# mLSTM cell and mixture of depths on one core: another order of work within a chunk

## The chip, the core and the metric

The kernel runs on one core of a Trainium2 chip. A core has five engines that run their own instruction queues in order: TensorE (PE in the profile, its weight loads PEld), VectorE (DVE), ScalarE (ACT), GpSimd (POOL) and SyncE (SP), which here only starts DMA transfers. They meet through semaphores. The metric is the device time of one execution in microseconds.

## The reference

Two stages in a row. The first is an mLSTM cell over 4 batches, 8 heads, 768 tokens and a head size of 40; its output, heads side by side, is a row of 320 per token. The second picks in every batch the 128 tokens with the highest score, and adds to each of these rows a gated two-layer network.

```python
# mLSTM, for every token t (B, H in front)
m_new  = max(f[t] + m, i[t])
f_stab = exp(f[t] + m - m_new);  i_stab = exp(i[t] - m_new);  m = m_new
C = f_stab * C + i_stab * outer(v[t], k[t])
n = f_stab * n + i_stab * k[t]
y[t] = sigmoid(o_gate[t]) * (C @ q[t]) / max(abs(n . q[t]), 1)

# mixture of depths, for every batch b, on x = y with the heads side by side (768 x 320)
scores = x @ w_gate
top = indices of the 128 largest scores
out = x
out[top] = x[top] + sigmoid(scores[top]) * (relu(x[top] @ w1) @ w2)     # w1 320x1024, w2 1024x320
```

## The kernel before

The tokens are cut into 24 chunks of 128: n = 6 b + c, chunk c of batch b. Within a chunk the recurrence is a masked 128 x 128 product per head; from chunk to chunk goes the state C. All products are float32. The gates of three chunks of all batches lie in one tile of 96 rows (chunk, batch, head), so there are two groups of them.

```python
def load_gates(eng, dst, src, g):                      # f_sb, i_sb: [96, 128]
    eng.dma_start(out=dst[g], in_=src.rearrange("b h (c p) -> c (b h) p", p=L)[3 * g:3 * g + 3])

load_gates(nc.sync, f_sb, f_gate, 0);   load_gates(nc.scalar, i_sb, i_gate, 0)
load_gates(nc.scalar, f_sb, f_gate, 1); load_gates(nc.scalar, i_sb, i_gate, 1)
...
def warm(n):                    # n fillers on TensorE: a bf16 product that nobody reads (pw)
def scans(g):                   # VectorE: running sums and maxima of the gates of a group (FM, a)
def ends(g), carry(g), carried(g), level(g, pm)        # the stabilizer m carried from chunk to chunk
def operands(u, c):             # TensorE pO, ScalarE a_o, VectorE M_o: factors whose product is log W
def turned(n):                  # TensorE transposes k and q (pt), ScalarE copies them (T)
def gated(n):                   # ScalarE: so = tanh(o_gate / 2) + 1
def weights(b, c):              # TensorE pW, ScalarE W = exp(pW), [128, 8, 128]
def causal(W):                  # GpSimd: affine_select zeroes W above the diagonal, in two halves
def scaled_v(b, c, v1):         # GpSimd: wv = v * column
def products(T):                # TensorE: pS = k q^T for 8 heads
def weighted(pS, W):            # VectorE: P = pS * W, in two halves
def decay(b, c):                # GpSimd: C of the next chunk = C * column
def exchange(b, c, qk, T, wv):  # TensorE: pI = C q, pC = k wv; VectorE: num = pI * column, then C += pC (c = 0: copy)
def within(P, v1):              # TensorE: pH = P v
...
def norm(num, pH, so):
    nc.vector.tensor_tensor(out=num, in0=num, in1=pH[:, :, 0:D1], op=OP.add)          # not for c = 0
    # two small VectorE operations: den = 2 max(|n q|, 1)
    nc.vector.reciprocal(out=rec, in_=den)
    nc.gpsimd.tensor_tensor(out=sor, in0=so, in1=rec.unsqueeze(2).to_broadcast([128, H, D]), op=OP.mult)
    return num, sor

def result(b, c, num, sor, sc):
    nc.vector.tensor_tensor(out=x..., in0=num[:, :, 0:D], in1=sor, op=OP.mult)
    nc.sync.dma_start(out=out[b, c * L:(c + 1) * L, :], in_=x)
    nc.vector.tensor_tensor_reduce(out=scr, in0=x, in1=wg, ..., accum_out=sc[:, c:c + 1])   # the score

def spread(u, sc, sb):          # TensorE pb, ScalarE sb: the scores of chunk u along the free axis
def compare(u, sc, sb, ge, cnt):# VectorE ge: which scores are at least as high, and how many
def columns_of(ge):             # TensorE pcol: 21 one-column products, counts the other way round
def ranks(pcol, cnt):           # two small VectorE operations
def select(sel, rank, t0, t1):  # VectorE: sel = (rank == 0 .. 127), 128 x 768
def gather(b, sel, token):      # TensorE pidx, VectorE idx, then GpSimd's indirect DMA: xe <- out[idx]

class Layers:                   # the two layers of one batch on its 128 rows
    def enter(self):            # TensorE pX (transposes of xe), ScalarE xeT
    def gate(self):             # VectorE scre, ScalarE exp, VectorE +1 and reciprocal
    def first(self, f0, f1):    # TensorE ph, ScalarE relu hT after every fourth f; 8 f in all
    def second(self, f0, f1):   # TensorE py
    def leave(self):            # VectorE ye, GpSimd's indirect DMA: out[idx] <- ye
```

The step of one chunk, in the order of each engine's queue:

```python
def ranking(b, c):
    if b > 0 and c == 1:
        rank = ranks(columns_of(state[b - 1][1][2]), state[b - 1][1][3])
        select(sel[b - 1], rank, 0, NT)
    elif b > 0 and c == 2:
        picked[b - 1] = gather(b - 1, sel[b - 1], token)

def layer(b, c):
    if c < 3:
        if b > 1:  layers[b - 2].second(3 * c, min(3 * c + 3, NFC))
        else:      warm(3)
    elif b == 0:   warm(3)
    elif b < B - 1:
        if c > 3:  layers[b - 1].first(3 * c - 10, 3 * c - 7)
    elif c == 4:   layers[b - 1].first(2, 6)
    elif c == 5:
        layers[b - 1].first(6, NFC);  layers[b - 1].second(0, 4)

def entered(b, c):
    if b > 0 and c == 3:
        layers[b - 1] = Layers(b - 1, *picked[b - 1]);  layers[b - 1].enter();  layers[b - 1].first(0, 2)

def step(n):
    load(n + AHEAD)                                    # k, q, v, o_gate of chunk n + 4: four DMAs
    P = weighted(pS[n], W[n])
    W[n + 2] = weights(*steps[n + 2])
    num = exchange(b, c, qk, T[n], wv[n])
    ranking(b, c);  layer(b, c)
    pH = within(P, v1)
    spread(pc, ...)                                    # of the chunk before
    turned(n + 2);  gated(n + 2)
    pS[n + 1] = products(T[n + 1])
    num, sor = norm(num, pH, so)
    decay(*steps[n + 1])
    causal(W[n + 2]);  stated(n + 2)                   # stated: scaled_v
    compare(pc, ...)                                   # of the chunk before
    result(b, c, num, sor, state[b][0])
    entered(b, c)
    if b > 0 and c == 3:  layers[b - 1].gate()
    if b > 1 and c == 2:  layers[b - 2].leave()
    if n + 3 < NT:        operands(0, n + 3)
    if 3 <= n < 3 + NT:   operands(1, n - 3)
```

Ahead of the steps stands a start with the work of chunk 0 and the gates; behind them a tail: the last spread and compare, `own.second(4, NFC)` of batch 2, ranks, select, products with sel, the gather and both layers of batch 3, and the last scatter.

Of the kernel before, what the change touches and what calls it, by code (L numbers as in the profile page):

```python
# [27 lines left out]
def kernel(  # L28
# [59 lines left out]
    i_sb = [gate.tile([NR, L], FP, name=f"i_sb{g}") for g in range(2)]  # L88

    def load_gates(eng, dst, src, g):  # L90
        eng.dma_start(out=dst[g], in_=src.rearrange("b h (c p) -> c (b h) p", p=L)[3 * g:3 * g + 3])

    load_gates(nc.sync, f_sb, f_gate, 0)
    load_gates(nc.scalar, i_sb, i_gate, 0)
    load_gates(nc.scalar, f_sb, f_gate, 1)
    load_gates(nc.scalar, i_sb, i_gate, 1)
    earlier = const.tile([128, NT * L], BF, name="earlier")
    nc.gpsimd.memset(earlier, 1.0)
    ident = const.tile([128, 128], FP, name="ident")
# [69 lines left out]
    def warm(n):  # L169

        pw = ps_h.tile([128, 4 * L], FP, name="pw", tag="h")
        for _ in range(n):
            nc.tensor.matmul(pw, earlier[:, 0:128], earlier[:, 0:4 * L], start=True, stop=True)  # L173
# [233 lines left out]
    def columns_of(ge):  # L407

        pcol = ps_m.tile([128, NT], FP, name="pcol", tag="m")
        for t in reversed(range(NT)):  # L410
            for u in reversed(range(t, NT)):
                nc.tensor.matmul(pcol[:, t:t + 1], ge[:, GE[u] + t * L:GE[u] + (t + 1) * L], ones_b, start=(u == NT - 1),
                                 stop=(u == t))
        return pcol

    def ranks(pcol, cnt):


        rank = mod.tile([128, NT], FP, name="rank")
        nc.vector.tensor_tensor(out=rank, in0=cnt, in1=later, op=OP.add)  # L420
        nc.vector.tensor_tensor(out=rank, in0=rank, in1=pcol, op=OP.subtract)
        return rank

    def select(sel, rank, t0, t1):
        nc.vector.tensor_tensor(out=sel[:, t0:t1], in0=iota_f.unsqueeze(1).to_broadcast([128, t1 - t0, K_]),
                                in1=rank[:, t0:t1].unsqueeze(2).to_broadcast([128, t1 - t0, K_]), op=OP.is_equal)

    def gather(b, sel, token):
        pidx = ps_m.tile([K_, 1], FP, name="pidx", tag="m")
        for t in range(NT):  # L430
            nc.tensor.matmul(pidx, sel[:, t, :], token[:, t:t + 1], start=(t == 0), stop=(t == NT - 1))
        idx = mod.tile([K_, 1], U32, name="idx")
        nc.vector.tensor_scalar(out=idx, in0=pidx, scalar1=float(b * S), scalar2=None, op0=OP.add)
        xe = xe_t[b % 2]
        nc.gpsimd.indirect_dma_start(out=xe[0:K_, 0:DM], out_offset=None, in_=rows(b),
                                     in_offset=bass.IndirectOffsetOnAxis(ap=idx, axis=0),
                                     bounds_check=(b + 1) * S - 1, oob_is_err=False)
        return idx, xe

    class Layers:  # L440
# [14 lines left out]
        def gate(self):  # L455
            scr = mod.tile([K_, DM], FP, name="scre", bufs=1)
            self.g = g = mod.tile([K_, 1], FP, name="g")
            nc.vector.tensor_tensor_reduce(out=scr, in0=self.xe[0:K_, 0:DM], in1=wg[0:K_], scale=1.0, scalar=0.0,
                                           op0=OP.mult, op1=OP.add, accum_out=g)
            nc.scalar.activation(out=g, in_=g, func=AF.Exp, scale=-1.0)  # L460
            nc.vector.tensor_scalar(out=g, in0=g, scalar1=1.0, scalar2=None, op0=OP.add)
            nc.vector.reciprocal(out=g, in_=g)

        def first(self, f0, f1):
            for f in range(f0, f1):
# [41 lines left out]
    def stated(n):  # L507
        wv[n] = scaled_v(*steps[n], loaded[n][1])

    def ranking(b, c):  # L510

        if b > 0 and c == 1:
            rank = ranks(columns_of(state[b - 1][1][2]), state[b - 1][1][3])
            sel[b - 1] = mod.tile([128, NT, K_], HF, name="sel", bufs=1)
            select(sel[b - 1], rank, 0, NT)
        elif b > 0 and c == 2:
            picked[b - 1] = gather(b - 1, sel[b - 1], token)

    def layer(b, c):
# [17 lines left out]
    def entered(b, c):  # L537
        if b > 0 and c == 3:
            layers[b - 1] = Layers(b - 1, *picked[b - 1])
            layers[b - 1].enter()  # L540
            layers[b - 1].first(0, 2)

    def step(n):
        b, c = steps[n]
        qk, v1, so = loaded[n]
        load(n + AHEAD)
        P = weighted(pS[n], W[n])
        if n + 2 < N:
            W[n + 2] = weights(*steps[n + 2])
        num = exchange(b, c, qk, T[n], wv[n])  # L550
        ranking(b, c)
        layer(b, c)
        pH = within(P, v1)
# [8 lines left out]
        if n + 1 < N:  # L562
            decay(*steps[n + 1])
        if n + 2 < N:
# [7 lines left out]
        if b > 0 and c == 3:  # L572
# [12 lines left out]
    load(2)  # L585
    load(3)
    load(4)
    pS = {}
    warm(7)

    scans(0)
    ends(0)
    split(0, 1, 0, nc.vector.tensor_copy, nc.vector)
    carry(0)
    warm(2)
    pm = carried(0)
    split(0, 1, 1, nc.vector.tensor_copy, nc.vector)
# [4 lines left out]
    turn(loaded[0][0], 0, T[0])  # L602
    operands(0, 0)
    scales(0)
    turn(loaded[0][0], 1, T[0])
    warm(1)
    W[0] = weights(0, 0)
    pS[0] = products(T[0])
    operands(0, 1)
    columns(0)  # L610
    warm(2)
    causal(W[0])
    stated(0)

    gated(0)
    scans(1)
    W[1] = weights(0, 1)
    P = weighted(pS[0], W[0])
    split(1, 1, 0, nc.gpsimd.tensor_copy, nc.gpsimd)
    split(1, 1, 1, nc.gpsimd.tensor_copy, nc.gpsimd)  # L620
    ends(1)
    warm(2)
    exchange(0, 0, loaded[0][0], T[0], wv[0])
    carry(1)
    turned(1)
    operands(0, 2)
    causal(W[1])
    stated(1)
    pm = carried(1)
    pH = within(P, loaded[0][1])  # L630
    pS[1] = products(T[1])
    level(1, pm)
    W[2] = weights(0, 2)
    num, sor = norm(None, pH, loaded[0][2])
    split(1, 0, 0, nc.scalar.copy, nc.vector)
    decay(0, 1)
    causal(W[2])
    stated(2)
    split(1, 0, 1, nc.scalar.copy, nc.vector)
    result(0, 0, num, sor, state[0][0])  # L640
    scales(1)
    gated(1)
    turned(2)
# [89 lines left out]
```

## Time and profile before

| | |
|---|---|
| time, median of 3 runs | 234.72 us (232.8 to 236.89) |
| span of the profiled execution | 235.5 us |
| mean granted TensorE clock | 0.896 |
| first pH after the start (chunk 0) | 23.46 us |
| pH of chunk 6, 12, 18 | 77.22, 124.64, 166.89 us |
| last spread (pb) | 208.51 us |

Busy time is given by engine, and in windows by stage. A row of a group tells the line of the kernel, the engine, the operation, what it writes and reads (names of tiles), the shapes, how often, then busy microseconds and the mean in nanoseconds of one, then the time that the engine had stood idle ahead of it and what ended that. The chain of work goes back from the last instruction, at each step to what released it; a piece has its start, its length and what it was.

### The profile page before, as it was taken

The numbers are of one execution on the slowest core, as the hardware profiler recorded it, in microseconds if no ns is written. First come the engines' busy times: TensorE is split into PE (matmuls) and PEld (weight loads), VectorE is DVE, ScalarE is ACT, GpSimd is POOL, SyncE is SP. The second block draws the span as 40 slices with busy tenths as digits, with TensorE's granted clock in tenths as the row PEclk, the third lists the DMA queues.
The fourth block names the chain that finished last, engine by engine and source line by source line (L and its number), as shares of the span: only waits on it lengthen the run. The fifth ranks groups of instructions, "written<-read, shape, count | busy, mean of one in ns | idle before, by whom it ended". The sixth has DMA issues, their size and how long they took to land.

```text
span 235.5 us, 6469 instructions
## 1 busy us (share of the span) xinstructions
PE 201.2 (85%) x2611; PEld 159.6 (68%) x2611; DVE 156.0 (66%) x414; ACT 93.9 (40%) x212; POOL 104.6 (44%) x152
## 2 busy tenths in 40 slices
PE   5799889669778898589999997999999799858991
PEld 1356757457556886477887776788787679637980
DVE  3644273875888898886678789857888885642010
ACT  3643282343355353533565344465434541100020
POOL 6035320860556536731546477534647951021101
PEclk9755556997999799979999999999999999958998
DMA  4899964748599999999089987949992110000100
GB/s 72 144 159 148 98 101 42 112 76 97 154 132 200 157 212 190 152 125 140 25 120 140 144 125 135 168 53 141 131 134 49 58 57 3 28 31 29 30 0 28
DMA packets 105674, 24.37 MB, mean 103 GB/s; under 512 B 100460, under 2 KB 105068, under 8 KB 105644
## 3 DMA queue, kind: packets, MB, share of 16 engines
q1 hardware_dynamic: 104963, 22.50, 65.4%
q0 software_dynamic: 384, 1.31, 2.0%
q8 instruction: 20, 0.33, 0.7%
q10 hardware_dynamic: 297, 0.15, 0.2%
q14 instruction: 10, 0.08, 0.1%
HBM read 19.37 MB, written 4.59 MB: 102 GB/s over the span
## 4 chain that ended last, share of the span: by engine, by line
PE 58%; DVE 15%; issue 13%; POOL 5%; DMA 4%; ACT 2%; POOLq 1%
PE pH L367 12%; PE pS L313 9%; PE ph L469 8%; PE pt L271 7%; PE pIC L339 5%; PE py L478 4%; DVE x L387 4%; PE pIC L345 3%; PE pw L173 3%; POOL sor L382 2%; PE pW L291 2%; DVE scr L390 2%; DMA f_sb<-in_f_gate_dram 2%; PE pb L396 2%; DVE P L319 2%
## 5 line engine op out<-in xcount | busy, mean ns | idle before, releaser
L382 POOL TENSOR_TENSOR sor<-so,rec 128x320 f32<-128x320 f32 x24 | 23.3, 969 | 87.5 <-DVE rec L380 82.2
L367 PEld LDWEIGHTS pH<-v,P 128*64 128x64 f32 x768 | 28.4, 153 | 21.0 <-DVE P L319 8.3
L367 PE MATMUL pH<-v,P 128*64 128x64 f32 x768 | 32.0, 242 | 11.9 <-DVE P L319 6.0
L297 POOL TENSOR_SCALAR_AFFINE_SELECT W<-W 128x512 f32<-128x512 f32 x48 | 37.1, 794 | 9.1 <-ACT W L292 9.1
L397 ACT COPY sb<-pb 128x128 f32<-128x128 f32 x24 | 6.4, 266 | 71.4 <-PE pb L396 71.4
L292 ACT ACTIVATE W<-pW 128x512 f32<-128x512 f32 x48 | 26.0, 594 | 12.0 <-PE pW L291 7.6
L319 DVE TENSOR_TENSOR P<-pS,W 128x512 f32<-128x512 f32 x48 | 30.6, 677 | 0.0
L272 ACT COPY T<-pt 128x512 f32<-128x512 f32 x48 | 26.1, 588 | 9.9 <-PE pt L271 9.9
L313 PE MATMUL pS<-T 64*128 64x128 f32 x384 | 29.7, 297 | 0.0
L271 PE MATMUL pt<-ident,qk 128*128 128x128 f32 x192 | 29.0, 300 | 0.7 <-ACT W L292 0.7
L387 DVE TENSOR_TENSOR x<-num,sor 128x320 f32<-128x320 f32 x20 | 20.3, 1017 | 12.5 <-POOL sor L382 12.5
L313 PEld LDWEIGHTS pS<-T 64*128 64x128 f32 x384 | 24.9, 199 | 4.6 <-issue 4.4
L271 PEld LDWEIGHTS pt<-ident,qk 128*128 128x128 f32 x192 | 24.9, 156 | 1.7 <-ACT W L292 1.2
L469 PE MATMUL ph<-xeT,w 128*128 128x128 f32 x192 | 24.1, 280 | 2.0 <-ACT xeT L453 1.7
L469 PEld LDWEIGHTS ph<-xeT,w 128*128 128x128 f32 x192 | 22.2, 192 | 3.3 <-ACT xeT L453 2.4
L478 PE MATMUL py<-w,hT 128*128 128x320 f32 x64 | 21.4, 480 | 0.0
L374 DVE TENSOR_TENSOR num<-num,pH 128x328 f32<-128x328 f32 x20 | 9.9, 496 | 16.2 <-PE pH L367 16.0
L390 DVE CUSTOM_DVE_ANT_0 scr<-x,wg 128x320 f32<-128x320 f32 x24 | 17.1, 712 | 0.8
L304 POOL TENSOR_TENSOR wv<-v,cols 128x328 f32<-128x328 f32 x20 | 16.2, 811 | 2.6 <-DVE cols L245 2.6
L403 DVE SCALAR_TENSOR_TENSOR ge<-sb,sc,earlier 128x128 bf16<-128x128 f32 (+5 forms) x24 | 16.0, 667 | 1.0 <-ACT sb L397 0.9
L339 PE MATMUL pIC<-C,T 128*64 128x82 f32 x320 | 16.4, 246 | 0.0
L339 PEld LDWEIGHTS pIC<-C,T 128*64 128x64 f32 x320 | 13.0, 140 | 4.1 <-issue 2.5
(124 smaller groups left out, 269.5 us busy)
## 6 DMA issues: line engine op xcount, KB each, us to landing
qk<-in_k_dram SPq DMA_DIRECT2D x24, 160.0 KB, 3.8
qk<-in_q_dram SPq DMA_DIRECT2D x24, 160.0 KB, 5.0
v<-in_v_dram SPq DMA_DIRECT2D x24, 160.0 KB, 4.9
so<-in_o_gate_dram SPq DMA_DIRECT2D x24, 160.0 KB, 4.5
out_dram<-x SPq DMA_DIRECT2D x24, 160.0 KB, 1.9
w<-in_moe_w_dram SPq DMA_DIRECT2D x2, 640.0 KB, 4.5
w<-in_moe_w_dram SPq DMA_DIRECT2D x2, 512.0 KB, 4.0
w<-in_moe_w_dram SPq DMA_DIRECT2D x1, 256.0 KB, 3.9
```

The costliest lines, as they stand in the source:

```text
L271: nc.tensor.transpose(pt[:, p, :], qk[:, j, 2 * p:2 * p + 2, :].rearrange("s a d -> s (a d)"), ident)
L272: nc.scalar.copy(out=T[:, j], in_=pt)
L292: nc.scalar.activation(out=W[:, h0:h0 + 4, :], in_=pW, func=AF.Exp)
L297: nc.gpsimd.affine_select(out=W[:, h0:h0 + 4, :], in_=W[:, h0:h0 + 4, :], compare_op=OP.is_ge, fill=0.0, base=0, pattern=[[0, 4], [1, L]], ...
L313: nc.tensor.matmul(pS[j][:, p, :], T[e, 0, p, :], T[e, 1, p, :], start=True, stop=True)
L319: nc.vector.tensor_tensor(out=P[:, :, j, :], in0=pS[j], op=OP.mult, in1=W.rearrange("p (n a) t -> p n a t", a=2)[:, :, j, :])
L339: nc.tensor.matmul(pI[t, 2 * p * D1:2 * (p + 1) * D1], T[:, 1, p, t], C[:, p].rearrange("e a d -> e (a d)"), start=True, stop=True)
L367: nc.tensor.matmul(pH[t, 2 * p + j, :], P[:, p, j, t], v1[:, 2 * p + j, :], start=True, stop=True)
L382: nc.gpsimd.tensor_tensor(out=sor, in0=so, in1=rec.unsqueeze(2).to_broadcast([128, H, D]), op=OP.mult)
L387: nc.vector.tensor_tensor(out=x.rearrange("p (h d) -> p h d", d=D), in0=num[:, :, 0:D], in1=sor, op=OP.mult)
L469: nc.tensor.matmul(self.ph[:, f % 4, :], w1[:, j, f * 128:(f + 1) * 128], self.xeT[:, j, :], start=(j == 0), stop=(j == NDC - 1))
L478: nc.tensor.matmul(self.py, self.hT[:, f, :], w2[:, f, :], start=(f == 0), stop=(f == NFC - 1))
```

## The change

The order within a chunk changes, and with it the place of the second stage's work. GpSimd does the selects, wv and the decay of the state as soon as their inputs can be there, and the product with the output gate, sor, last. The ranking of a batch goes to the end of the next batch's chunk 0 (it was in chunk 1), the gather to chunk 1 (2), the entry of the layers and the gate to chunk 2 (3); the closing two operations of the gate become `gated()`, at chunk 3. The first layer then takes chunks 3 to 5. The last batch does five second products ahead of the tail instead of four. The gates are loaded in pieces of 32 rows, the second group by SyncE behind chunk 0. In the start VectorE's operations of chunk 0 take another order, and the fillers stand elsewhere.

```diff
     def load_gates(eng, dst, src, g):
-        eng.dma_start(out=dst[g], in_=src.rearrange("b h (c p) -> c (b h) p", p=L)[3 * g:3 * g + 3])
+        for c in range(3):
+            t = slice((3 * g + c) * L, (3 * g + c + 1) * L)
+            eng.dma_start(out=dst[g][c * BH:(c + 1) * BH], in_=src[:, :, t].rearrange("b h p -> (b h) p"))
 ...
-    load_gates(nc.scalar, f_sb, f_gate, 1)
-    load_gates(nc.scalar, i_sb, i_gate, 1)
 ...
-    def ranking(b, c):
+    def layer(b, c):
         if b > 0 and c == 1:
-            rank = ranks(columns_of(state[b - 1][1][2]), state[b - 1][1][3])
-            sel[b - 1] = mod.tile([128, NT, K_], HF, name="sel", bufs=1)
-            select(sel[b - 1], rank, 0, NT)
+            picked[b - 1] = gather(b - 1, sel[b - 1], token)
         elif b > 0 and c == 2:
-            picked[b - 1] = gather(b - 1, sel[b - 1], token)
+            layers[b - 1] = Layers(b - 1, *picked[b - 1])
+            layers[b - 1].enter()
         if c < 3: ...                                   # as before
         elif b == 0:
             warm(3)
+        elif c == 3:
+            layers[b - 1].gated()
+            layers[b - 1].first(0, 3)
         elif b < B - 1:
-            if c > 3:
-                layers[b - 1].first(3 * c - 10, 3 * c - 7)
+            layers[b - 1].first(3 * c - 9, min(3 * c - 6, NFC))
         elif c == 4:
-            layers[b - 1].first(2, 6)
-        elif c == 5:
-            layers[b - 1].first(6, NFC)
-            layers[b - 1].second(0, 4)
-    def entered(b, c): ...
+            layers[b - 1].first(3, 7)
+        else:
+            layers[b - 1].first(7, NFC)
+            layers[b - 1].second(0, 5)
 ...
     def step(n):
         P = weighted(pS[n], W[n])
             W[n + 2] = weights(*steps[n + 2])
+            causal(W[n + 2])
+            stated(n + 2)
         num = exchange(b, c, qk, T[n], wv[n])
-        ranking(b, c)
+            decay(*steps[n + 1])
         layer(b, c)
         ...
             pS[n + 1] = products(T[n + 1])
         num, sor = norm(num, pH, so)
-            decay(*steps[n + 1])
-            causal(W[n + 2])
-            stated(n + 2)
         compare(pc, *state[pb][1])
+        if b > 0 and c == 0:
+            pcol = columns_of(state[b - 1][1][2])
         result(b, c, num, sor, state[b][0])
-        entered(b, c)
-        if b > 0 and c == 3:
+        if b > 0 and c == 0:
+            rank = ranks(pcol, state[b - 1][1][3])
+            sel[b - 1] = mod.tile([128, NT, K_], HF, name="sel", bufs=1)
+            select(sel[b - 1], rank, 0, NT)
+        elif b > 0 and c == 2:
             layers[b - 1].gate()
-        if b > 1 and c == 2:
-            layers[b - 2].leave()
+            if b > 1:
+                layers[b - 2].leave()
 ...
     load(0)
+    load_gates(nc.sync, f_sb, f_gate, 1)
+    load_gates(nc.sync, i_sb, i_gate, 1)
     load(1)
 ...                                                     # the start: fillers warm(...) in order
-    warm(7); scans; ends; split; carry; warm(2); carried; ...; turn; operands; scales; turn; warm(1); weights; products; columns; warm(2)
+    warm(8); scans; ends; warm(2); split; carry; carried; warm(1); ...; turn; warm(1); operands; scales; turn; columns; weights; warm(1); products
 ...                                                     # chunk 0: P ahead of W[1], causal(W[1]) and turned(1) ahead of exchange,
-    scans(1); W[1] = weights(0, 1); P = weighted(...); split; ends(1); warm(2); exchange(0, 0, ...); carry(1); turned(1); ...
+    scans(1); P = weighted(...); W[1] = weights(0, 1); split; causal(W[1]); ends(1); turned(1); warm(1); exchange(0, 0, ...); carry(1); ...
 ...                                                     # the tail
-    own.second(4, NFC)
+    own.second(5, NFC)
     last.gate()
+    last.gated()
```

More of the change, by code (lines that the diff above doesn't have):

```diff
@@ L460, in gate, with gated @@
             nc.scalar.activation(out=g, in_=g, func=AF.Exp, scale=-1.0)
-            nc.vector.tensor_scalar(out=g, in0=g, scalar1=1.0, scalar2=None, op0=OP.add)
-            nc.vector.reciprocal(out=g, in_=g)
+        def gated(self):
+            nc.vector.tensor_scalar(out=self.g, in0=self.g, scalar1=1.0, scalar2=None, op0=OP.add)
+            nc.vector.reciprocal(out=self.g, in_=self.g)
         def first(self, f0, f1):
@@ L508, in stated @@
         wv[n] = scaled_v(*steps[n], loaded[n][1])
-    def ranking(b, c):
+    def layer(b, c):
         if b > 0 and c == 1:
-            rank = ranks(columns_of(state[b - 1][1][2]), state[b - 1][1][3])
-            sel[b - 1] = mod.tile([128, NT, K_], HF, name="sel", bufs=1)
-            select(sel[b - 1], rank, 0, NT)
+            picked[b - 1] = gather(b - 1, sel[b - 1], token)
         elif b > 0 and c == 2:
-            picked[b - 1] = gather(b - 1, sel[b - 1], token)
-    def layer(b, c):
+            layers[b - 1] = Layers(b - 1, *picked[b - 1])
+            layers[b - 1].enter()
         if c < 3:
@@ L527, in layer @@
             warm(3)
+        elif c == 3:
+            layers[b - 1].gated()
+            layers[b - 1].first(0, 3)
         elif b < B - 1:
-            if c > 3:
-                layers[b - 1].first(3 * c - 10, 3 * c - 7)
+            layers[b - 1].first(3 * c - 9, min(3 * c - 6, NFC))
         elif c == 4:
-            layers[b - 1].first(2, 6)
-        elif c == 5:
-            layers[b - 1].first(6, NFC)
-            layers[b - 1].second(0, 4)
-    def entered(b, c):
-        if b > 0 and c == 3:
-            layers[b - 1] = Layers(b - 1, *picked[b - 1])
-            layers[b - 1].enter()
-            layers[b - 1].first(0, 2)
+            layers[b - 1].first(3, 7)
+        else:
+            layers[b - 1].first(7, NFC)
+            layers[b - 1].second(0, 5)
     def step(n):
@@ L549, in step @@
             W[n + 2] = weights(*steps[n + 2])
+            causal(W[n + 2])
+            stated(n + 2)
         num = exchange(b, c, qk, T[n], wv[n])
-        ranking(b, c)
+        if n + 1 < N:
+            decay(*steps[n + 1])
         layer(b, c)
@@ L561, in step @@
         num, sor = norm(num, pH, so)
-        if n + 1 < N:
-            decay(*steps[n + 1])
-        if n + 2 < N:
-            causal(W[n + 2])
-            stated(n + 2)
         compare(pc, *state[pb][1])
+        if b > 0 and c == 0:
+            pcol = columns_of(state[b - 1][1][2])
         if c == 0:
@@ L570, in step @@
         result(b, c, num, sor, state[b][0])
-        entered(b, c)
-        if b > 0 and c == 3:
+        if b > 0 and c == 0:
[3 more added lines that the diff above has]
+        elif b > 0 and c == 2:
             layers[b - 1].gate()
-        if b > 1 and c == 2:
-            layers[b - 2].leave()
+            if b > 1:
+                layers[b - 2].leave()
         if n + 3 < NT:
@@ L588 @@
     pS = {}
-    warm(7)
+    warm(8)
     scans(0)
     ends(0)
+    warm(2)
     split(0, 1, 0, nc.vector.tensor_copy, nc.vector)
     carry(0)
-    warm(2)
     pm = carried(0)
+    warm(1)
     split(0, 1, 1, nc.vector.tensor_copy, nc.vector)
@@ L602 @@
     turn(loaded[0][0], 0, T[0])
+    warm(1)
     operands(0, 0)
@@ L605 @@
     turn(loaded[0][0], 1, T[0])
+    columns(0)
+    W[0] = weights(0, 0)
     warm(1)
-    W[0] = weights(0, 0)
     pS[0] = products(T[0])
     operands(0, 1)
-    columns(0)
-    warm(2)
     causal(W[0])
@@ L616 @@
     scans(1)
+    P = weighted(pS[0], W[0])
     W[1] = weights(0, 1)
-    P = weighted(pS[0], W[0])
     split(1, 1, 0, nc.gpsimd.tensor_copy, nc.gpsimd)
     split(1, 1, 1, nc.gpsimd.tensor_copy, nc.gpsimd)
+    causal(W[1])
     ends(1)
-    warm(2)
+    turned(1)
+    warm(1)
     exchange(0, 0, loaded[0][0], T[0], wv[0])
     carry(1)
-    turned(1)
+    pH = within(P, loaded[0][1])
     operands(0, 2)
-    causal(W[1])
+    pm = carried(1)
+    pS[1] = products(T[1])
+    num, sor = norm(None, pH, loaded[0][2])
     stated(1)
-    pm = carried(1)
-    pH = within(P, loaded[0][1])
-    pS[1] = products(T[1])
+    decay(0, 1)
     level(1, pm)
     W[2] = weights(0, 2)
-    num, sor = norm(None, pH, loaded[0][2])
     split(1, 0, 0, nc.scalar.copy, nc.vector)
-    decay(0, 1)
+    result(0, 0, num, sor, state[0][0])
+    split(1, 0, 1, nc.scalar.copy, nc.vector)
     causal(W[2])
     stated(2)
-    split(1, 0, 1, nc.scalar.copy, nc.vector)
-    result(0, 0, num, sor, state[0][0])
     scales(1)
```

## The prediction

> **What bounds the kernel now.** I read the page first, then the chain of work that ended last in order of time, the groups by line with shapes kept apart, and the windows by stage, and I followed a few steps of one 128-token chunk instruction by instruction. The page says which engine is fullest, and that the granted TensorE clock is half in the slices from about 12 to 35 us:
>
> ```profile
> PE 201.2 (85%) x2611; PEld 159.6 (68%) x2611; DVE 156.0 (66%) x414; ACT 93.9 (40%) x212; POOL 104.6 (44%) x152
> ...
> PEclk9755556997999799979999999999999999958998
> ```
>
> The stages follow (columns: length, busy time of each engine, granted clock, DMA). "Chunk n" is the n-th of 24; the boundaries are starts of pH.
>
> ```profile
> 0.00:37.40 37.40, 30.32 (x217) 18.76 (x217) 18.40 (x59) 16.97 (x39) 12.79 (x32) 0.62 0.96 120
> ...
> 55.60:92.10 36.50, 30.77 (x497) 24.96 (x498) 29.92 (x75) 17.25 (x40) 19.91 (x28) 0.94 0.98 155
> 92.10:124.60 32.50, 28.49 (x395) 24.20 (x395) 25.00 (x61) 15.20 (x33) 14.92 (x18) 0.95 0.80 127
> 124.60:166.90 42.30, 40.28 (x611) 33.39 (x610) 34.13 (x90) 21.10 (x46) 24.36 (x29) 1.00 0.86 126
> ```
>
> From 124.6 us on PE is 95% busy: little is left there. From 37 to 124 it is not, although it runs three filler matmuls (pw) per chunk that compute nothing. The chain shows why; this is chunk 4 to chunk 5:
>
> ```profile
> 67.98 0.77 PE pw L173 x3
> 68.75 1.58 issue
> 70.33 1.24 PE pH L367 x32
> ```
>
> PE stands 1.58 us in front of pH, which needs P = pS x W from VectorE. So this stage is **VectorE's loop**: P, num, C, then num+pH, den, rec, ge, a wait for GpSimd's sor, x, scr, and P again. Two members of it are stretched:
>
> ```profile
> L387 DVE TENSOR_TENSOR x<-num,sor 128x320 f32<-128x320 f32 x20 | 20.3, 1017 | 12.5 <-POOL sor L382 12.5
> L387 DVE TENSOR_TENSOR x<-pH,sor 128x320 f32<-128x320 f32 x4 | 1.9, 485 | 1.2 <-POOL sor L382 1.2
> L390 DVE CUSTOM_DVE_ANT_0 scr<-x,wg 128x320 f32<-128x320 f32 x24 | 17.1, 712 | 0.8
> ```
>
> The same x takes 1017 ns with both inputs in SBUF and 485 ns with one in PSUM; in chunk 22, where GpSimd has nothing left to do, the SBUF form takes 0.49 too. GpSimd works exactly there because its queue runs sor, decay (C), two affine selects (W), wv, and sor waits for rec: 82.2 us of waiting in all, after which everything behind it falls on x and scr. Worst is chunk 8, behind the gather:
>
> ```profile
> 96.03 2.89 DVE x L387
> 98.92 0.03 issue
> 98.95 0.49 DVE scr L390
> ```
>
> PE idles 3.44 us there, and the next matmuls come out at half clock (pt x8 takes 1.70 instead of 0.87).
>
> **What the Trainium skill says.** GPSIMD Engine Reference, Key points: GpSimd shares its SBUF interfaces with VectorE, and they contend when the VectorE instruction has two SBUF inputs. The trace agrees (1017 against 485 ns). DMA: Bandwidth & Descriptors, the section on why a DMA increments its semaphore by 16: a DMA is spread over the largest k up to 16 that divides the slowest dimensions of both sides. The old gate load has 3 on one side and 96 on the other, which would be 3 engines; its 48 KB take 4.65 us on the chain, 160 KB of x take 1.9 to land. The trace agrees without showing the engines. TensorE: Matmul & The Clock Gate, What's actually happening: half clock after an idle window of about 3.4 us, full after a busy one. The trace agrees loosely: half from 8.9 to 39.6 us although PE is about 90% busy by the page's modelled ends, so the threshold can't be read off it. The DMA page, Issuing engines are not separate DMA queues: moving the second gate loads from ScalarE to SyncE changes only who spends the issue time, seen here as 0.4 to 1.9 us an issue.
>
> **The change, part by part**, from 234.7 us.
>
> *GpSimd's order.* The selects, wv and decay come ahead of sor. They need W of chunk n+2 (ScalarE ends it about 1 us after the old sor ends) and C of this chunk, so they fall under P, num and C, which have one input in PSUM. Their sum is 1.5 + 0.74 + 0.73 = 3.0 us, begun some 3.2 us after one pH ends, done before the next rec. Then x falls from 1.01 to 0.49 and scr from 0.80 to 0.49: 0.83 us per chunk in VectorE's loop (0.7 where there is no decay). sor beside ge (0.72 alone, up to 1.39) stays. Chunks 1 to 8 run on that loop or on the similar one through M_o and pW (in chunks 1 and 2): seven intervals, 54.7 us, at 0.83 = 5.8; another 0.7 for half-clock pieces (75 to 80 us stands at 0.72) as PE idles less: **-6.5**.
>
> *Chunks 8 to 12 of batch 1.* x of 2.88 loses 2.4 (0.49 left), and the half-clock matmuls of 100.8 to 104.6 lose 1.5 (pH 0.6, pt 0.8, pb 0.1). The entry of the layers moves a chunk forward, so PE no longer waits 0.57 for xeT, which ScalarE copies while PE has its transposes. Two more exposed waits of about 0.3 are worth 0.5: **-5**. As a check, PE's need here is four times 4.7 plus 6.4 of first, 1.7 of second, under 27 against 32.6 used.
>
> *Batches 2 and 3.* Ranks and select (0.17 + 0.17 + 0.96 = 1.3 us of VectorE) move from chunk 1 to chunk 0, which has no num and so a light VectorE; the gather moves to chunk 1, the entry to chunk 2; the gate keeps its 0.9 scre but leaves chunk 3. Exposed now per batch: 1.28 in front of pH of chunk 3, 0.57 for xeT, 0.16 for idx, 2.0 together, twice 4.0. The gather is issued after C and lands 3.4 us later, about 4 us before pX wants it. After the change VectorE needs about 5.5 us from pH of chunk 2 to P, PE 6.1 (0.2 + 0.87 + 1.09 + 0.32 + 1.18 + 2.4 of first), so PE waits no more. Less half a microsecond for the fifth second matmul moved in, and half kept for leftovers: **-3**.
>
> *The tail.* One of four second matmuls leaves the stretch at half clock (208.5 to 212.5): two passes at 0.53, **-1**. The rest of the tail is as it was.
>
> *The start.* The gates load as 3 DMAs of 32 rows. Three issues of some 0.65 end at 2.8, landing some 1.9 later gives 4.6 against 5.46: **-1**. The fillers are moved (14 to 14) to where PE idled between the gate steps (4.8 to 6.8 us); if this keeps the full clock, the 27 us of PE work from 9 to 37 shrink towards 14, but six gate loads now stand ahead of chunk 1 on SyncE, some 3 to 4 us of issue, so chunk 1 lands near 18 us rather than 15, and its transposes (20.3 now) can't come much before. Possible gain 0 to 6, taken as **-2**.
>
> Sum: 6.5 + 5 + 3 + 1 + 1 + 2 = 18.5. I give back 2 for waits I can't see, so 234.7 - 16.5: **218 us**.
>
> **Rivals.** *One: the contention only moves.* W of chunk n+2 may be ready as x starts, and then the selects sit on scr again. For it: ScalarE ends W only about half a microsecond after x's new end. In the late chunks, with ge long and sor late, part of it must happen. Against: a select has one input and stretches scr by 0.3 only; decay, the one that stops x, now waits for C. If x and scr stay long, the middle gives 4 instead of 11.5 and the time is about 225. *Two: the late sor becomes the bound*, as GpSimd reaches it only after selects, wv, decay, and in chunk 1 the 1.05 us gather. For it: GpSimd has 3.0 to 4.1 us of work within an interval of 6. Against: it has waited 2 to 6 us for rec in nearly every chunk. Cost: up to 0.5 in the three chunks with a gather, 219.5; if it hit 20 chunks, 228. *Three: the start binds on data or clock.* Chunk 1 or the second gates come late behind each other on SyncE, VectorE stops in scans(1), PE idles: the start loses 2 to 3 instead of winning 3, and the time is about 223. The reverse, full clock all through the start, gains 6 instead of 2 and gives 214. *Four: PE hides it all.* Only from 124 us on, where PE is 95% busy; counted.
>
> **Range and chances.** The middle (11.5) rests on measured durations and the chain, so some gain is nearly sure; its size depends on how soon PE takes over as the bound, and on the clock at the start. 209 has the warm start (4 less), no unseen waits (2 less), nothing left over in batches 2 and 3; 228 has rival one with a bad start. The runs of before spread from 232.8 to 236.9 by themselves. Over 2% faster means below 230.0: 0.88. Within 2%: 0.09. Slower: 0.03, if a buffer or queue order makes a wait per chunk that I overlooked.
>
> **What would show it.** Right: x with both inputs in SBUF near 0.5 us and scr near 0.5; GpSimd's wait for rec now at the end of its queue with sor starting about 0.1 after rec; pH's waits in chunks 3 to 8 under 0.8 us; no x of 2.9; intervals of about 6.2 us there and of 40.5 us per batch later; f_sb on the chain under 4 us; six py passes after the last spread instead of eight. Wrong: x still near 1 us; sor waiting for C or W instead of rec; pH still behind P by 1.5; scans(1) or pt waiting for a DMA; half clock in more slices than before. The prediction fails altogether if the middle gains under 4 us.

## The result

The changed kernel takes 216.79 us in the median of four runs (216.01 to 222.25), the one before 234.91. The ratio is 0.9245, with a 95% interval of 0.9161 to 0.933. The profiled execution has a span of 214.3 us against 235.5.

### The profile page after: what moved, and what is told of

The parts are those of the page before. It is cut to its first block, busy times and chain, and to the rows that moved or that the text cites. A ratio compares the mean times of both kernels' runs of the same rounds, so it can differ in the third digit from the quotient of the medians.

```text
span 214.3 us, 6507 instructions
## 1 busy us (share of the span) xinstructions
PE 187.8 (88%) x2611; PEld 150.9 (70%) x2611; DVE 139.3 (65%) x414; ACT 93.9 (44%) x212; POOL 99.2 (46%) x152
## 4 chain that ended last, share of the span: by engine, by line
PE 59%; DVE 14%; issue 11%; DMA 6%; POOL 5%; ACT 2%; POOLq 1%; SPq 0%; DVEq 0%
PE pH L367 12%; PE ph L471 8%; PE pS L313 8%; PE pt L271 6%; PE py L480 6%; PE pIC L339 5%; POOL sor L382 4%; DMA xe<-out_dram,idx 4%; PE pIC L345 3%; PE pw L173 3%; PE pW L291 3%; PE pb L396 2%; DVE x L387 2%; DVE scr L390 2%; DVE num L374 1%
## 5 line engine op out<-in xcount | busy, mean ns | idle before, releaser
L382 POOL TENSOR_TENSOR sor<-so,rec 128x320 f32<-128x320 f32 x24 | 24.1, 1006 | 47.5 <-DVE rec L380 43.2
L297 POOL TENSOR_SCALAR_AFFINE_SELECT W<-W 128x512 f32<-128x512 f32 x48 | 31.5, 678 | 29.9 <-ACT W L292 29.9
L367 PEld LDWEIGHTS pH<-v,P 128*64 128x64 f32 x768 | 26.2, 145 | 11.8 <-PE pw L173 5.7
L367 PE MATMUL pH<-v,P 128*64 128x64 f32 x768 | 29.4, 233 | 3.4 <-PE pw L173 1.6
L313 PE MATMUL pS<-T 64*128 64x128 f32 x384 | 27.9, 285 | 0.0
L313 PEld LDWEIGHTS pS<-T 64*128 64x128 f32 x384 | 23.3, 187 | 3.9 <-issue 3.8
L271 PE MATMUL pt<-ident,qk 128*128 128x128 f32 x192 | 25.3, 274 | 0.7 <-ACT W L292 0.7
L374 DVE TENSOR_TENSOR num<-num,pH 128x328 f32<-128x328 f32 x20 | 9.9, 496 | 21.2 <-PE pH L367 21.1
L271 PEld LDWEIGHTS pt<-ident,qk 128*128 128x128 f32 x192 | 21.6, 140 | 1.5 <-ACT W L292 1.0
L387 DVE TENSOR_TENSOR x<-num,sor 128x320 f32<-128x320 f32 x20 | 9.8, 492 | 13.2 <-POOL sor L382 13.2
L480 PEld LDWEIGHTS py<-w,hT 128*128 128x128 f32 x64 | 12.1, 200 | 4.1 <-issue 0.6
L327 POOL TENSOR_TENSOR C<-C,cols 128x328 f32<-128x328 f32 x16 | 11.8, 735 | 6.7 <-DVE C L359 5.7
```

The lines of the kernel that those rows point to most:

```text
L271: nc.tensor.transpose(pt[:, p, :], qk[:, j, 2 * p:2 * p + 2, :].rearrange("s a d -> s (a d)"), ident)
L297: nc.gpsimd.affine_select(out=W[:, h0:h0 + 4, :], in_=W[:, h0:h0 + 4, :], compare_op=OP.is_ge, fill=0.0, base=0, pattern=[[0, 4], [1, L]], ...
L313: nc.tensor.matmul(pS[j][:, p, :], T[e, 0, p, :], T[e, 1, p, :], start=True, stop=True)
L367: nc.tensor.matmul(pH[t, 2 * p + j, :], P[:, p, j, t], v1[:, 2 * p + j, :], start=True, stop=True)
L480: nc.tensor.matmul(self.py, self.hT[:, f, :], w2[:, f, :], start=(f == 0), stop=(f == NFC - 1))
```

## The profile after

The same views as before. The page: VectorE loses 17 us of busy time for the same 414 instructions, TensorE 13 us for the same 2611, and the half clock of 12 to 35 us is gone but for two short pieces.

```profile
PE 187.8 (88%) x2611; PEld 150.9 (70%) x2611; DVE 139.3 (65%) x414; ACT 93.9 (44%) x212; POOL 99.2 (46%) x152
...
PEclk9997889999999997999999999999999999969998
```

The windows by stage, cut at the starts of pH of chunks 0, 1, 8, 12 and 18 (length, busy times, granted clock, DMA):

```profile
0.00:16.07 16.07, 12.50 (x99) 7.05 (x101) 9.86 (x35) 10.52 (x23) 8.22 (x25) 0.97 0.87 122
16.07:29.31 13.24, 10.31 (x121) 7.42 (x119) 8.55 (x24) 6.49 (x16) 6.72 (x11) 0.78 1.19 157
29.31:81.66 52.35, 42.55 (x699) 33.20 (x699) 39.50 (x110) 24.99 (x57) 29.47 (x48) 0.98 0.99 162
81.66:108.78 27.12, 27.02 (x392) 23.22 (x392) 18.97 (x57) 14.45 (x32) 11.48 (x16) 0.97 0.87 122
108.78:148.76 39.98, 39.65 (x609) 33.26 (x608) 29.65 (x90) 21.14 (x46) 22.73 (x30) 1.00 0.85 134
```

From chunk 8 to chunk 23 TensorE is 99% busy. The chain from chunk 4 to chunk 5, where pH stood 1.58 us for P, now has 0.87 (ahead of chunk 4 it still has 1.53, taken up below):

```profile
55.94 0.77 PE pw L173 x3
56.71 0.87 issue
57.58 1.26 PE pH L367 x32
```

The two stretched VectorE operations, from the instructions that touch x (minimum, median and maximum in ns):

```profile
L390 DVE CUSTOM_DVE_ANT_0 scr<-x,wg x24: 491/492/800, 22.8 to 188.1; 128x320 f32<-128x320 f32 x24
...
L387 DVE TENSOR_TENSOR x<-num,sor x20: 491/492/494, 32.5 to 187.6; 128x320 f32<-128x320 f32 x20
```

None of the 20 is above 494 ns. GpSimd in chunks 13 and 14 shows why (start, length, operation; in brackets the idle time ahead of it and what ended that): the selects, wv and C lie between two sor, and sor comes last and waits for rec.

```profile
118.96 0.71 POOL L382 TENSOR_TENSOR sor<-so,rec 128x320 f32<-128x320 f32 x1 [0.18 <-issue]
120.97 1.22 POOL L297 TENSOR_SCALAR_AFFINE_SELECT W<-W 128x512 f32<-128x512 f32 x2 [1.30 <-ACT W L292]
122.16 0.74 POOL L304 TENSOR_TENSOR wv<-v,cols 128x328 f32<-128x328 f32 x1
123.05 0.74 POOL L327 TENSOR_TENSOR C<-C,cols 128x328 f32<-128x328 f32 x1 [0.15 <-DVE C L359]
125.30 0.85 POOL L382 TENSOR_TENSOR sor<-so,rec 128x320 f32<-128x320 f32 x1 [1.50 <-DVE rec L380]
```

There is also a wait that was not there before. The chain, in chunks 7 and 8 (the tokens of batch 0 are gathered in chunk 7 and wanted in chunk 8):

```profile
73.65 5.88 DMA xe<-out_dram,idx
79.52 0.14 issue
79.66 0.66 PE pX L451 x3
```

and among the waits (total, how often, longest):

```profile
POOL sor L382 <- DVE rec L380: 43.2, 19, 6.4
POOL W L297 <- ACT W L292: 29.9, 20, 5.4
...
PE pX L451 <- DMA xe<-out_dram,idx: 3.5, 1, 3.5
```

This table splits all profiled executions of the study at starts of pH, in us. It is the base of what follows; the runs' medians are given with each experiment.

| kernel | to pH of chunk 1 | 1 to 7 | 7 to 8 | 8 to 12 | 12 to 23 | 23 to the end | span |
|---|---|---|---|---|---|---|---|
| before | 37.4 | 47.7 | 7.0 | 32.6 | 79.0 | 31.8 | 235.5 |
| changed | 29.3 | 41.9 | 10.5 | 27.1 | 75.1 | 30.4 | 214.3 |
| GpSimd's order only | 37.2 | 42.4 | 7.2 | 31.3 | 76.9 | 32.1 | 227.2 |
| start only | 32.9 | 45.8 | 7.5 | 32.7 | 79.0 | 33.2 | 231.1 |
| layers only | 37.5 | 48.6 | 8.7 | 28.5 | 78.9 | 29.0 | 231.2 |
| changed, sor first | 30.6 | 48.7 | 7.6 | 28.0 | 77.3 | 32.5 | 224.5 |
| changed, gates in one DMA | 34.4 | 42.5 | 11.0 | 27.3 | 75.1 | 31.5 | 221.9 |
| changed, no fillers at the gates | 31.5 | 42.6 | 10.8 | 27.5 | 75.3 | 31.6 | 219.2 |
| changed, w2 later | 31.2 | 42.7 | 7.5 | 26.6 | 75.2 | 32.7 | 215.9 |
| changed, entry later | 30.6 | 43.7 | 7.2 | 28.2 | 75.1 | 32.7 | 217.5 |
| changed, on a second chip | 32.9 | 42.6 | 10.7 | 27.5 | 75.1 | 31.5 | 220.3 |
| w2 later and tail | 32.9 | 42.4 | 9.4 | 28.0 | 75.1 | 29.0 | 216.8 |
| more fillers in the start | 26.9 | 43.1 | 10.8 | 28.0 | 75.4 | 28.9 | 213.2 |
| all three | 26.6 | 43.3 | 7.7 | 26.4 | 75.1 | 28.9 | 208.0 |

One kernel's runs differ by 2 to 6 us, as TensorE's clock falls at other places from run to run; medians are over all runs, ratios over the undisturbed ones.

## Experiments: one part at a time

**GpSimd's order only**, on the kernel before:

```diff
             W[n + 2] = weights(*steps[n + 2])
+            causal(W[n + 2]);  stated(n + 2)
         num = exchange(b, c, qk, T[n], wv[n])
+        decay(*steps[n + 1])
 ...
         num, sor = norm(num, pH, so)
-        decay(*steps[n + 1]);  causal(W[n + 2]);  stated(n + 2)
```

> The kernel before with one thing of the change: selects, wv and decay ahead of sor on GpSimd. Start, fillers, ranking, gather and layers as before. Theory (each part pays by itself, this one most): x with both inputs in SBUF falls from 1017 to about 492 ns, scr to about 495, the 2.88 us x of chunk 8 is gone; chunks 1 to 12 give 8 to 10 us and the later ones 1 to 2, so about 224 to 226. Rival (the new order pays only together with the moved layers, which take the load off VectorE in chunks 1 to 3): x and scr get as short, but the time stays above 230.

Measured: 227.41 us (225.24 to 228.93) against 236.12 on its chip, ratio 0.961 (0.952 to 0.970). All 20 x are short here too:

```profile
L387 DVE TENSOR_TENSOR x<-num,sor x20: 491/492/493, 40.5 to 198.8; 128x320 f32<-128x320 f32 x20
```

It gives 5.3 us in chunks 1 to 7, 1.3 in 8 to 12 and 2.1 later: chunks 1 to 12 bring 6.3 where 8 to 10 were expected. The rival falls, as this part pays without the others; by the medians it is also the largest of the three, though the runs of the next part spread too far to rank it.

**Start only**: the gates in pieces, the second group on SyncE, fillers and order of chunk 0 of the changed kernel; the 23 later chunks as before.

> The kernel before with the start of the changed one: gates in pieces of 32 rows, second group behind chunk 0, fillers and the order of chunk 0; all 23 later chunks as before. Theory: the first pH comes at 16 us instead of 23.5, the whole 7 to 8 us stay to the end: 226 to 228. Rival (the later stages have their own bound and swallow the lead, because loads or GpSimd aren't ready): pH of chunk 6 is less than 4 us earlier than the 77.2 of before, and the time is above 231.

Measured: 233.18 us (227.85 to 233.71) against 236.12; the expected 226 to 228 came in one run of four. pH of chunk 0 comes at 17.9, that of chunk 1 only 4.5 us earlier than before, as the clock is half from about 14 to 34 us in this execution. The lead of 4.5 is kept: pH of chunk 6 is at 72.3 against 77.2, so the stages between swallow nothing; the time above 231 is the rival's, its reason is not. The run at 227.85 has a mean clock of 0.952 over the span, the others 0.914.

**Layers only**: ranking, gather, entry, gate and first/second products moved, all else as before.

> The kernel before with the moved ranking, gather, entry, gate and first/second products, and nothing else. Theory: it removes the 0.57 us wait for xeT and the wait in front of pH of chunk 3 in each batch and a microsecond in the tail, but adds a wait for the gathered rows in batch 1, as these are wanted one chunk after the gather: minus 1 to minus 4 in all, 231 to 234. Rival (the move is what frees VectorE in chunks 1 to 3 and makes the change): 228 or less.

Measured: 232.89 us (230.52 to 237.15, 20 runs), ratio 0.993 (0.988 to 0.998). The small gain is a sum of large terms: 4.1 us less in chunks 8 to 12, 2.8 less after chunk 23, where the clock was full in this execution, and 2.6 more in chunks 1 to 8 (1.5 of that is TensorE's wait for the gathered rows). The rival falls. The long x of 2.88 us is gone here too, although sor still stands first on GpSimd:

```profile
L387 DVE TENSOR_TENSOR x<-num,sor x20: 491/1008/1014, 41.0 to 205.9; 128x320 f32<-128x320 f32 x20
```

**Changed kernel with sor first** (the inverse of the first diff):

> The changed kernel with the old order on GpSimd: sor first, then decay, selects, wv. Theory: x back at about 1.0 us and scr at 0.8 where GpSimd works, VectorE's loop 0.8 us longer per chunk until chunk 12 and in chunk 2 of later batches: 8 to 11 us more than the changed kernel, 225 to 228. Rival (the layers' move and the start carry the gain): 221 or less.

Measured: 226.68 us (226.23 to 227.16), as expected, ratio to before 0.962 (0.954 to 0.969). From the page:

```profile
L387 DVE TENSOR_TENSOR x<-num,sor 128x320 f32<-128x320 f32 x20 | 18.5, 924 | 12.3 <-POOL sor L382 12.3
L390 DVE CUSTOM_DVE_ANT_0 scr<-x,wg 128x320 f32<-128x320 f32 x24 | 17.4, 726 | 0.8
```

Taken away last, GpSimd's order is worth 226.7 less 216.8 to 219.3 (the changed kernel on two chips), 7.4 to 9.9 us; put in first it was worth 8.7. So it stands nearly by itself. By stages it is 6.8 us in chunks 1 to 7 and 2.2 in 12 to 23; between chunks 7 and 8 the old order is even shorter, as the rows are waited for less there (1.3 us).

## Experiments: the start

**Gates in one DMA each**, at the places of the changed kernel:

```diff
-        for c in range(3):
-            t = slice((3 * g + c) * L, (3 * g + c + 1) * L)
-            eng.dma_start(out=dst[g][c * BH:(c + 1) * BH], in_=src[:, :, t].rearrange("b h p -> (b h) p"))
+        eng.dma_start(out=dst[g], in_=src.rearrange("b h (c p) -> c (b h) p", p=L)[3 * g:3 * g + 3])
```

> The changed kernel with each gate load as one DMA again (slowest dimension 3), at the same places in the queues. Theory (the pieces bring the gates 1.7 us earlier: first scan at 3.76 against 5.46): the first scan is back at about 5.4, the first pH about 1.7 us later and the time 218 to 219. Rival (the early gates are also what keeps TensorE's clock up at the start): half clock from about 9 us, first pH above 20 us, time above 221.

Measured: 224.4 us (222.86 to 224.74). The rival's signs all came. The first scan is at 5.47 as expected (first line the changed kernel, second this run), but the clock is half again from 8.5 us:

```profile
3.76 0.42 DVE L177 TENSOR_TENSOR_SCAN FM<-earlier,f_sb 96x128 f32<-96x128 bf16 x1 [0.75 <-DMA f_sb<-in_f_gate_dram]
5.47 0.42 DVE L175 TENSOR_TENSOR_SCAN FM<-earlier,f_sb 96x128 f32<-96x128 bf16 x1 [2.46 <-DMA f_sb<-in_f_gate_dram]
...
8.50:22.10 13.60, 12.21 (x92) 8.56 (x91) 5.91 (x16) 6.65 (x14) 4.71 (x9) 0.50 1.17 154
```

and pH of chunk 0 comes at 21.1 instead of 16.1. The second group's scan, too, waits for a DMA until 16.26 (12.39 in the changed kernel); how much of the 5 us is that and how much the clock was not separated.

**No fillers at the gates**: the six of the changed start are left out, the first eight stay.

> The changed kernel without the six fillers that stand between the gate steps and chunk 0's products (2, 1, 1, 1, 1); the first eight stay. Theory (the fillers keep the clock): the half clock starts near 9 us instead of 15, the first pH comes at 19 to 21 us instead of 16, time 219 to 222. Rival (early gates and order carry the start): first pH at 16 to 17, time 216 to 217.5.

Measured: 221.72 us (219.06 to 222.68). The clock is half from 9.2 to 19.4 us, pH of chunk 0 at 18.1; the expected 19 to 21 was a little too late.

```profile
9.20:19.40 10.20, 8.85 (x81) 6.79 (x82) 4.40 (x11) 4.93 (x10) 4.72 (x9) 0.50 1.30 160
```

TensorE is 87% busy there and keeps half clock all the same. The fillers stand ahead of this stretch, and with them the half clock begins at 15.2 us. Why is not shown: without them TensorE is busy for 80% of the time from 4.1 to 9.2 us instead of 93%, but its longest idle time there is only 0.49 us. How much these six are worth stays open as well, as the changed kernel was not run beside them.

## Experiments: the wait for the gathered rows

**w2 two chunks later.** At the gather of batch 0 a load of 640 KB of w2 and the next chunk's loads are in the DMA queues.

```diff
-        elif 3 + NDC <= n < 5 + NDC:
-            load_w2(n - 3 - NDC)
+        elif 5 + NDC <= n < 7 + NDC:
+            load_w2(n - 5 - NDC)
```

> The changed kernel with the two loads of w2 (640 KB each) issued two chunks later, so that none of them is in the DMA queues when the first gather is issued; nothing needs w2 before chunk 12. Theory (the gathered rows come late because 16 DMA engines are busy with w2 and the next chunk): the rows land in about 3.4 us instead of 5.9, TensorE's 3.5 us in front of pX shrink below 1, time 213 to 215. Rival (the gather is slow by itself in its first use, or the next chunk's loads alone hold it up): 5 us or more, time 216 to 217.

Measured: 216.6 us (214.47 to 217.58). The rows land within 3.6 us, and

```profile
PE pX L451 <- DMA xe<-out_dram,idx: 1.3, 1, 1.3
```

The interval from chunk 7 to 8 falls from 10.5 to 7.5, as the theory says. The time does not show it: the same profile has 1.9 us more ahead of chunk 1 and 2.3 more after chunk 23, where TensorE's clock fell earlier. So the load of w2 is shown to be most of the wait, and the gather isn't slow by being the first. It isn't all: pX still waits 1.3 us, and 2.2 in another execution with w2 moved (below). The worth in the run's time isn't shown by this run.

**Entry one chunk later** for batch 0 only:

```diff
             layers[b - 1] = Layers(b - 1, *picked[b - 1])
-            layers[b - 1].enter()
+            if b > 1:
+                layers[b - 1].enter()
 ...
         elif c == 3:
+            if b == 1:
+                layers[b - 1].enter()
             layers[b - 1].gated()
```

> The changed kernel, but batch 0's rows are transposed (pX) at the start of chunk 9 instead of chunk 8; the later batches as in the change. Theory (the 3.5 us wait in front of pX is on the path): the interval from chunk 7 to 8 falls from 10.5 to about 7, half a microsecond comes back as TensorE's wait for xeT, time 213.5 to 215. Rival (VectorE binds there anyway, or the time returns in front of the next pH): 216 to 217.

Measured: 217.9 us (215.49 to 219.62), inconclusive as a time. From chunk 7 to 8 it is 7.2 us, but from 8 to 9 it is 9.3 instead of 8.2, with 0.8 of waiting for xeT and 0.5 for a_o in front of pX: a third of the gain comes back at once. By these intervals loading w2 later is the better cure (chunk 8 to 9 takes 7.7 there).

## Experiments: what they add up to

The changed kernel again, as the base on this chip:

> The changed kernel itself, on the same chip as the three that follow, as their base. Expected 216 to 217.5; single runs near 222 where TensorE's clock falls early.

Measured: 219.28 us (217.46 to 222.07) against 237.21, ratio 0.934 (0.926 to 0.942), above the expected 216 to 217.5. The instructions are those of the 216.79 above. The profile has the reason for the higher end:

```profile
PEclk9975558999999995999999999999999999966998
...
13.00:33.00 20.00, 16.95 (x150) 12.57 (x152) 10.88 (x30) 9.10 (x21) 9.60 (x17) 0.52 1.07 153
```

Half clock for about 20 us, where the first profile of the same kernel had two pieces of 3 us; pH of chunk 1 comes at 32.9 instead of 29.3.

**w2 later and the tail**: besides the w2 loads,

```diff
+    own.second(5, NFC)
+    warm(6)
     spread(u, sc, sb)
     compare(u, sc, sb, ge, cnt)
-    own.second(5, NFC)
+    warm(4)
     rank = ranks(columns_of(ge), cnt)
```

> The changed kernel with w2 loaded two chunks later, and in the tail the last three second products ahead of the last spread, with 6 and 4 fillers around that spread. Theory (the wait for the gathered rows is on the path at 3.0 us, and the half clock of the tail is worth another 1.5 to 3): 211 to 213. Rival (what is saved early is lost to the clock again, as the first w2 run's gain was): 215 or more.

Measured: 216.6 us (214.04 to 218.49), ratio 0.920 (0.911 to 0.930), 2.7 us below the base, short of the 211 to 213 and where the rival put it. The start has the same half clock as the base's (chunk 1 at 32.9), the gather took 4.6 us and pX waited 2.2. The tail takes 29.0 us against 31.5.

**More fillers in the start**: 13 of them where TensorE waits for M_o, FM and T.

```diff
     P = weighted(pS[0], W[0])
+    warm(3)
     W[1] = weights(0, 1)
+    warm(2)
 ...
     turned(2)
+    warm(4)
     operands(0, 3)
+    warm(4)
     columns(1)
```

> The changed kernel with 13 more fillers in the start, where TensorE waits for M_o, FM and T (about 12, 13.3, 23 and 24.5 us). Theory (the clock falls because these waits leave too little work in a stretch): half clock below 1 us in all of the first 40 us, the second pH 2 to 3 us earlier than the changed kernel's 29.3 or the spread of the runs smaller, 213.5 to 215. Rival (fillers get in the way of real work and VectorE's chain sets the pace there): 216 to 218.

Measured: 214.93 us (213.37 to 216.83), ratio 0.917 (0.909 to 0.925), 4.3 us below the base. pH of chunk 1 at 26.9. The windows (chunk 0's and chunk 1's pH lie at 16.1 and 26.9):

```profile
0.00:16.00 16.00, 13.73 (x99) 7.00 (x102) 9.94 (x35) 10.35 (x23) 7.66 (x24) 1.00 0.86 122
16.00:27.00 11.00, 9.53 (x136) 6.22 (x135) 8.17 (x24) 6.56 (x17) 6.58 (x12) 1.00 1.21 147
27.00:40.00 13.00, 11.16 (x162) 9.08 (x164) 8.06 (x26) 5.96 (x14) 7.85 (x16) 0.87 1.03 135
```

The clock is full through the start, and the fillers are in nobody's way; the half clock is put off to a piece after 27 us, not abolished. All six runs lie below all six of the base, so on this chip the fillers pay. The tail of this execution takes 28.9 us with the tail unchanged, at full clock, like the 29.0 of layers only; so about 28.9 is what the tail needs at full clock with or without the edit. That the edit makes full clock likelier is not shown: two of the nine tails without it have it, and both with it.

**All three**:

> The changed kernel with all three: w2 later, the tail, and the fillers at the start. If the three are independent: 208 to 211; if the clock at the start costs as much as before, 212 to 213.

Measured: 210.88 us (209.7 to 212.08), ratio to before 0.901 (0.894 to 0.909), 8.4 us below the changed kernel on the same chip and within the 208 to 211 of independent parts. The runs lie within 2.4 us.

```profile
PEclk9999999789999999999999999999999999999998
```

## Why the prediction was right, and where not

The time was foretold as 218 us, from 234.7, and the measured one is 216.79, from 234.91. The stages, from the spans of the two profiles, say how far that was earned:

| stage | predicted | by the profiles |
|---|---|---|
| start, to pH of chunk 1 | -3 | -8.1 |
| chunks 1 to 8 | -6.5 | -2.3 |
| chunks 8 to 12 | -5 | -5.5 |
| chunks 12 to 23 | -3 | -3.9 |
| tail | -1 | -1.4 |
| given back for waits not seen | +2 | |
| sum | -16.5 | -21.2 |

The sum is nearer than its terms. The start brought 5.1 us more than foretold, and the wait for the gathered rows took 4.2 of what chunks 1 to 8 should have brought: that the two nearly cancel is luck. In the second profile of the same kernel the start brought 4.5. The ends of the range are looser than the sum, too: the three terms named for 209 lead to about 211.

**GpSimd's order: right in mechanism and in sum, not in its even steps.** x and scr fall to 492 ns, and chunks 1 to 7 lose 5.8 us against six times 0.83, 5.0, and 0.7 for the clock. The part alone and the part taken away (8.7 and 7.4 to 9.9 us) show it. What the Trainium skill (GPSIMD Engine Reference, Key points) says of two SBUF inputs agrees with all 20 x: before, 18 are long, and the two short ones have no work of GpSimd beside them; after, all are short. But the six intervals lose 1.7, 1.8, 0.5, 0.7, 0.7 and 0.4 us. Part of the first terms is the clock: three fillers ahead of chunk 3 take 1.41 us before and 0.77 after. And in chunk 3 rival one came true, the contention only moved: two small set-up operations of VectorE with one input each, which make token and later, now run beside GpSimd's selects and wv and take 0.62 and 0.61 us instead of 0.22 and 0.17. P starts 3.07 us after x there, 3.06 before, and pH of chunk 4 waits as long as ever:

```profile
49.78 1.53 issue
51.31 1.24 PE pH L367 x32
```

So two of the prediction's signs failed: this wait isn't under 0.8, and intervals of about 6.2 us came in chunks 4 and 5 only, 7.3 to 7.4 in the four others from chunk 1 to 7. Otherwise rival one fell: scr keeps 0.8 in chunk 7 alone. Rival two fell: GpSimd still waits 43.2 us for rec; the exception is chunk 7, where the gather stands ahead of sor and x waits 1.68 us.

**The gather: the step that failed.** The prediction said that it "lands 3.4 us later, about 4 us before pX wants it". That was worked out for batches 2 and 3 and never asked of batch 1. In batch 2 the gather is issued at 117.73, takes 3.42 us, and pX runs at 121.32, so 0.2 us is spare (0.5 in batch 3), not 4. In batch 1 w2 is being loaded, it takes 5.88, and TensorE waits 3.5. The trace of before had the warning: its first gather takes 6.25 us, the later ones 2.9 to 3.8. This wait is the whole miss of chunks 1 to 8; w2 two chunks later takes 3.0 us of it away in that interval.

**Chunks 8 to 12: right sum, wrong share.** The 5 us were put down to GpSimd's order, which was to end the x of 2.88 us in chunk 8 and with it the half clock behind it (3.9 of 5). That step failed. GpSimd's order alone ends this x and gives 1.3 us in these chunks: x waits 1.53 us for sor, which still stands behind the gather, and the half clock comes all the same (chunk 9; this takes 1.04 at full clock):

```profile
95.64 1.91 PE L271 MATMUL pt<-ident,qk 128*128 128x128 f32 x8
```

The layers alone give 4.1, with no x above 1014 ns; the interval from chunk 9 to 10 falls from 11.2 to 7.0, where the entry was. Part of it is only moved: the layers alone pay 1.7 us between chunks 7 and 8. Why x took 2.88 us is not shown: in chunk 14 GpSimd ran gather, sor, C, W and wv without a gap as well, and there x took 1.01.

**Chunks 12 to 23: right sum, wrong share.** 39.98 us from chunk 12 to 18 where 40.5 was foretold. All of it was put down to the layers' move. GpSimd's order alone gives 2.1 of the 3.9; with the start and the layers but without the order it is 1.8. They add up. The layers alone show only 0.1, but the clock of that execution fell in chunk 12 (9.9 us to the next pH instead of 8.4).

**The start: a term mis-sized.** Three issues of a gate take 0.40 to 0.44 us each, not 0.65, so the first scan is at 3.76 instead of 5.46, 1.7 earlier and not 1. The Trainium skill (DMA: Bandwidth & Descriptors, on why a DMA increments its semaphore by 16) agrees with that: pieces of 32 rows can spread over more engines than a slowest dimension of 3; the engines themselves are not seen. Chunk 1's transposes run at 13.91 and wait for no DMA, as chunk 0's loads are issued in 2.6 us; "chunk 1 lands near 18" was wrong.

The full clock, taken as 2 of a possible 6, was worth more in one profile and little more in the next: pH of chunk 1 at 29.3 in one, at 32.9 in the other. Where the clock falls changes from one execution to the next, and here the prediction could give a range only. No run here shows the Trainium skill's rule (TensorE: Matmul & The Clock Gate, What's actually happening) by which an idle window of about 3.4 us brings the half clock: it came where the longest idle time of TensorE in the 5 us ahead was 0.49 us, and stretches that the profile shows 87 to 90% busy stayed at half.

**The tail: not shown.** One product less at half clock is 1.07 us on paper, and its sign came: six passes of py behind the last spread instead of eight. But with the same five second products the tail measures 28.9 to 32.7 us, by the clock, and two executions whose clock there was as low as before's (0.67 and 0.68 in its first 10 us, 0.66 before) take 32.5 and 32.7, no less than the 31.8 of before; 1.4 in one pair of profiles is no proof.

## What to carry to other kernels

An engine that is idle half of its time can still sit on the path: look at which two operations lie beside each other, and order its queue so that the work which contends falls beside operations that don't, the one-off ones included. When a consumer is moved forward, ask of each of its inputs, and of the first round apart from the steady ones, what else is in the DMA queues at that moment. And before a gain or loss of 2% is believed in a kernel of this length, look at the granted clock of the start and the tail; 13 fillers in the waits of the start brought 4.3 us.

## What the runs showed of the hardware

A VectorE operation with two SBUF inputs that starts as GpSimd goes on to the two-input decay takes 1.0 us instead of 0.49; x beside a select, which has one input, takes 0.90, scr 0.80. In chunk 8 x took 2.88 in two kernels (before and start only). With one input in PSUM x never changed (474 to 492 ns). Two small operations with one SBUF input took 0.6 us instead of 0.2 beside selects and wv. A gather of 128 rows takes 2.9 to 3.8 us to land in the later batches; the first takes 5.8 to 6.3 behind 640 KB of w2 and a chunk's loads, and 3.6 to 4.6 with w2 loaded later. The same instructions took 20 us at half clock in one execution and two pieces of 3 us in another, 220.3 and 214.3 us in all.
